# Batch 0's q in nine tokens per partition, as its k: two loads with longer rows, relu in halves, no separate tail

## Chip, cores and metric

The kernel runs on one core of one Trainium2 chip. The metric is the device time of one execution in microseconds (us), smaller is better. Each kernel was run several times; the text gives medians. A ratio is the mean time of one kernel's fast runs over that of the kernel before in the same rounds on the same chip, so not quite the ratio of the medians quoted.

## The reference

```python
def phi(x, c, s):                       # q and k: relu, then times cos and times sin
    r = np.maximum(x, 0.0)
    return np.concatenate([r * c, r * s], axis=-1)
kv  = einsum('bhsf,bhsd->bhfd', phi(k), v);  z = sum(phi(k), over tokens)
num = einsum('bhsf,bhfd->bhsd', phi(q), kv)
den = einsum('bhsf,bhf->bhs',   phi(q), z)[..., None] + 1e-6
x   = (num / den) as (4608 tokens, 512)         # 8 batches x 576 tokens, 8 heads x 64
xn  = x / sqrt(mean(x*x) + 1e-6) * rms_g
out = (silu(xn @ w_gate) * (xn @ w_val)) @ w_out        # 512 -> 1536 -> 512
```

q, k, v are float32 of shape (8, 8, 576, 64). The three matrix products of the last line are nearly all of TensorE's work. The scale c or s depends on the token alone.

## The kernel before

q is loaded with four tokens of one head per partition (512 of the 576 tokens), and the last 64 tokens, the tail, apart. k and v of batch 0 come with nine tokens per partition instead, as one contiguous run per partition. These loads all go through one queue (SyncE's) in the order of issue:

```python
def load_q_tokens(b, j0, j1):                   # before: 128 partitions x 8 heads
    view = q[b, :, 0:512, :].rearrange("h (p j) d -> p h j d", j=4)
    nc.sync.dma_start(out=raw[key][:, :, j0*D : j1*D],
                      in_=view[:, :, j0:j1, :].rearrange("p h j d -> p h (j d)"))
...
load_kv("k", 0, *LOW);  load_kv("k", 0, *HIGH)  # two halves of k
load_q_tokens(0, 0, 2)                          # q, tokens 0 and 1 of each four: 512 KB
first_v = load_kv("v", 0, *LOW)                 # ... then the rest of v in three loads
load_q_tokens(0, 2, 4)
```

Then, for a chunk c of 128 tokens of all heads: the relu with the scale (`q_phi`, once for cos on one engine and once for sin on the other), eight transposes on TensorE, an evacuation of the bank to SBUF, the product with kv and z (`nd_pe`), the division, the square and the norm (`x_sq`, `x_norm`), and the first products of the FFN:

```python
def q_phi(eng, b, c, part):
    src = view4(raw[("q", b)], c) if c < 4 else raw[("qt", b)][:, :, :]
    phi(eng, qp_tiles[(b, c)][:, :, o], src, f(c))          # one instruction of 512 elements
...                                                         # the opening, as issued:
    q_phi(A, 0, 2, 0); x_sq(0, 1)                           # chunk 2's relu ahead of a square
    ...
    q_phi(A, 0, 3, 1); q_tr_evac(A, 0, 2, psO[0][:, :])
    x_norm(0, 1)
    q_phi(V, 0, 3, 0)                                       # chunk 3's relu on DVE
    open_ffn(0, (0, 1), 0, 128)                             # the first FFN matmuls
    x_tr_pe(0, 1, psV[1][:, :]); x_tr_evac(V, 0, 1, psV[1][:, :])
    q_tr_pe(0, 3, psO[1][:, :])                             # chunk 3's transposes
```

In the profile's lines `phi` is L247 (ACT) and L249 (DVE), the copies and casts L316 and L318, the transposes of q L307, the first FFN matmuls L663. In the changed kernel the same lines are L252, L254, L337, L339, L321 and L692.

## Time and profile before

| | before |
|---|---|
| device time, first three runs | 327.01 us (326.49 to 327.02) |
| device time, six runs beside the changed kernel | 326.6 us (326.18 to 327.02) |
| profiled span | 325.4 us |
| PE busy / in the chain that ended last | 97% / 90% |
| first half of k, second half, q, first half of v land | 4.49, 6.03, 9.34, 10.86 us |
| first FFN matmul | 18.07 us |
| last weight load on PE, to the end of the span | 320.83 us, 4.62 us |

How to read it: PE works almost without a break from 18.07 us on, so a change in the opening can only move that start.

### The profile page before, as it was taken

To read this page: it belongs to the slowest core of one execution; us is meant where nothing else is said; L and a number is where in the kernel's file an instruction comes from. 1 tells how busy PE (TensorE), PEld (TensorE's weight loads), DVE (VectorE), ACT (ScalarE), POOL (GpSimd) and SP (SyncE) were. 2 spreads that over 40 slices of the span, in tenths; PEclk is the share of its full clock that TensorE was granted. 3 is DMA by queue.
4 is the path that set the end of the run, shared out by engine and by line. 5 is a ranking of instruction groups with operands and counts; after the bars stand their busy time and mean duration, and the time that the engine had idled before them with its cause. 6 is when DMAs were issued, how large, how long until landed. Compare 5 with 4: busy or idle time off the path is not lost.

```text
span 325.4 us, 6119 instructions
## 1 busy us (share of the span) xinstructions
PE 316.4 (97%) x2249; PEld 162.6 (50%) x2284; DVE 183.9 (57%) x394; ACT 173.4 (53%) x347; POOL 38.9 (12%) x85
## 2 busy tenths in 40 slices
PE   8999999999999999999999999999999999999994
PEld 3588465554445444554454445444544444444443
DVE  5875768787656765578267745772577143203310
ACT  6874775965665556645564466455654333233321
POOL 3570112001110110012001120120011000000000
PEclk9999999999999999999999999999999999999999
DMA  7999999887799665967597679766611400020014
GB/s 256 265 180 252 325 189 327 296 165 189 178 248 262 186 202 147 257 147 192 168 214 204 154 218 211 193 162 213 129 34 33 129 34 0 32 99 0 0 34 99
DMA packets 90881, 53.90 MB, mean 166 GB/s; under 512 B 56801, under 2 KB 83425, under 8 KB 90850
## 3 DMA queue, kind: packets, MB, share of 16 engines
q1 hardware_dynamic: 83808, 48.64, 57.3%
q0 software_dynamic: 6880, 4.72, 10.1%
q8 instruction: 18, 0.29, 0.4%
q10 hardware_dynamic: 162, 0.13, 0.2%
q14 instruction: 13, 0.11, 0.1%
HBM read 37.75 MB, written 9.44 MB: 145 GB/s over the span
## 4 chain that ended last, share of the span: by engine, by line
PE 90%; DMA 3%; ACT 2%; DVE 2%; issue 1%; SPq 0%; DVEq 0%
PE psC L544 26%; PE psV L524 26%; PE psG L524 26%; DMA rv<-in_v_dram 3%; PE psA L393 2%; PE psA L349 2%; PE psG L544 2%; PE psG L663 1%; PE psV L663 1%; PE psO L663 1%; PE psA L365 1%; ACT kpm L247 1%; PE psV L307 1%; ACT sg L533 0%; PE psA L400 0%
## 5 line engine op out<-in xcount | busy, mean ns | idle before, releaser
L539 DVE TENSOR_TENSOR hT<-psV,sg 128x512 bf16<-128x512 f32 x102 | 70.3, 689 | 95.9 <-PE psV L524 70.5
L533 ACT ACTIVATE sg<-psG 128x512 f32<-128x512 f32 x102 | 60.6, 594 | 64.9 <-PE psG L524 63.6
L524 PE MATMUL psV<-xnT,wv 128*128 128x512 bf16 (+1 forms) x365 | 92.1, 374 | 0.4
L524 PE MATMUL psG<-xnT,wg 128*128 128x512 bf16 (+1 forms) x352 | 90.8, 374 | 0.7
L544 PE MATMUL psC<-wo,hT 128*128 128x512 bf16 x382 | 88.2, 379 | 0.7
L524 PEld LDWEIGHTS <-wv 128*128 128x128 bf16 x416 | 40.6, 98 | 47.4
L544 PEld LDWEIGHTS <-hT 128*128 128x128 bf16 x420 | 40.3, 98 | 46.7
L524 PEld LDWEIGHTS <-wg 128*128 128x128 bf16 x416 | 38.6, 98 | 40.8 <-DVE xnT L318 0.4
L463 POOL TENSOR_TENSOR rs<-ms,mhalf 128x1 f32<-128x1 f32 x36 | 19.8, 549 | 187.9 <-ACT scr L458 187.9
L316 ACT COPY osb<-psC 128x512 f32<-128x512 f32 (+1 forms) x33 | 19.1, 578 | 43.4 <-PE psC L544 42.6
L485 DVE SCALAR_TENSOR_TENSOR xn<-xt,rs,gb 128x512 bf16<-128x512 f32 x35 | 26.5, 757 | 16.3 <-POOL rs L463 16.3
L458 ACT ACTIVATE scr<-xt 128x513 bf16<-128x513 f32 x36 | 22.8, 635 | 22.8 <-DVE xt L447 22.5
L247 ACT ACTIVATE kpm<-rk,tab 128x256 bf16<-128x256 f32 (+2 forms) x58 | 28.2, 545 | 1.7 <-DMA rk<-in_k_dram 1.7
L447 DVE TENSOR_TENSOR xt<-psA,rec 128x512 f32<-128x512 f32 x35 | 24.2, 691 | 1.2
L247 ACT ACTIVATE qp<-rq,tab 128x512 bf16<-128x512 f32 x32 | 22.4, 713 | 0.3 <-DMA rq<-in_q_dram 0.3
L249 DVE TENSOR_SCALAR kpm<-rk,tab 128x128 bf16<-128x128 f32 (+2 forms) x64 | 20.2, 374 | 2.3 <-DMA rk<-in_k_dram 2.3
L249 DVE TENSOR_SCALAR qp<-rq,tab 128x512 bf16<-128x512 f32 x32 | 15.3, 491 | 0.6 <-DMA rq<-in_q_dram 0.6
L393 PEld LDWEIGHTS <-qpT 128*128 128x128 bf16 x248 | 11.7, 98 | 6.7 <-issue 0.3
L393 PE MATMUL psA<-kvzs,qpT 128*128 128x65 bf16 x248 | 12.8, 193 | 0.3
L524 PE MATMUL psG<-xnt_tail,wg 128*128 128x512 bf16 x48 | 12.3, 379 | 0.1
L524 PE MATMUL psV<-xnt_tail,wv 128*128 128x512 bf16 x47 | 12.1, 379 | 0.0
L318 DVE CAST vvm<-rv 128x1024 bf16<-128x1024 f32 (+4 forms) x16 | 10.3, 670 | 0.2 <-DMA rv<-in_v_dram 0.2
(99 smaller groups left out, 184.3 us busy)
## 6 DMA issues: line engine op xcount, KB each, us to landing
out_dram<-osb SPq DMA_DIRECT2D x32, 256.0 KB, 2.6
rk<-in_k_dram SPq DMA_DIRECT2D x20, 256.0 KB, 3.4
rq<-in_q_dram SPq DMA_DIRECT2D x20, 256.0 KB, 3.0
rv<-in_v_dram SPq DMA_DIRECT2D x16, 256.0 KB, 3.1
rq<-in_q_dram SPq DMA_DIRECT2D x2, 1024.0 KB, 8.7
rv<-in_v_dram SPq DMA_DIRECT2D x3, 576.0 KB, 8.6
wo<-in_moe_w_out_dram POOLq DMA_DIRECT2D x4, 384.0 KB, 7.0
rk<-in_k_dram SPq DMA_DIRECT2D x2, 576.0 KB, 4.3
```

Of the source, the lines that this page charges most:

```text
L247: nc.scalar.activation(out=out_ap, in_=in_ap, func=AF.Relu, scale=scale)
L249: eng.tensor_scalar(out=out_ap, in0=in_ap, scalar1=scale, scalar2=0.0, op0=ALU.mult, op1=ALU.max)
L316: nc.scalar.copy(out=o, in_=i)
L393: nc.tensor.matmul(o[:, g, i, :], lhsT=qpT[(b, 0)][:, h, j * P : (j + 1) * P], rhs=kvz_of(b, h), start=True, stop=True,)
L447: nc.vector.tensor_tensor(out=xt[:, 0:DM].rearrange("p (b h d) -> p b h d", b=2, d=D), in0=o[:, :, :, 0:D], in1=rec[:, :, :].unsqueeze(3). ...
L458: nc.scalar.activation(out=scr[:, :], in_=xt[:, 0 : DM + 1], func=AF.Square, scale=1.0 / math.sqrt(DM), accum_out=ms[:, :],)
L463: nc.gpsimd.tensor_tensor(out=rs[:, :], in0=ms[:, :], in1=mhalf[:, :], op=ALU.pow)
L485: nc.vector.scalar_tensor_tensor(out=xn[:, :], in0=x_of[(b, j)][:, 0:DM], scalar=rs_of[(b, j)][:, :], in1=gb[:, :], op0=ALU.mult, op1=ALU. ...
L524: nc.tensor.matmul(pst[bank][:, cols[0] : cols[1]], lhsT=w[:, t, n * P : (n + 1) * P], rhs=x[:, t, cols[0] : cols[1]], start=(t == 0), sto ...
L533: nc.scalar.activation(out=sg[:, :], in_=psG[bank][:, :], func=AF.Silu)
L539: nc.vector.tensor_tensor(out=hTs[blk][:, n, :], in0=psV[bank][:, :], in1=sg[:, :], op=ALU.mult)
L544: nc.tensor.matmul(bank, lhsT=hTs[blk][:, n, j * P : (j + 1) * P], rhs=wo[:, n, :], start=(n == 0), stop=(n == NNT - 1),)
```

## The change

The intent: q of batch 0 in the layout of its k, so that its rows in DRAM are 1024 bytes (tokens 0 to 3 of nine) and 1280 bytes (tokens 4 to 8) instead of 512, and its tail needs no loads of its own. The price: a 64-row half of a chunk now holds another token, with another scale, so each relu becomes two instructions; the evacuation is strided; and block 0's rows are stored in eight pieces instead of four.

```diff
-    def load_q_tokens(b, j0, j1):
-        view = q[b, :, 0:512, :].rearrange("h (p j) d -> p h j d", j=4)
+    def load_q_tokens(j0, j1):
             out=raw[key][:, :, j0 * D : j1 * D],
-            in_=view[:, :, j0:j1, :].rearrange("p h j d -> p h (j d)"),
+            in_=q[0, :, :, :].rearrange("h s d -> (h s d)").rearrange(
+                "(r p n) -> p r n", p=P, n=NJ * D
+            )[:, :, j0 * D : j1 * D],
...
-    load_q_tokens(0, 0, 2)
+    load_q_tokens(0, 4)
     first_v = load_kv("v", 0, *LOW)
...
-    load_q_tokens(0, 2, 4)
+    load_q_tokens(4, NJ)
...  (q_phi)
+        if b == 0:
+            for i in range(2 if c < 4 else 1):
+                j = 2 * c + i
+                phi(eng, qp_tiles[(b, c)][:, 4 * i : 4 * i + 4, o],
+                    raw[("q", 0)][:, :, j * D : (j + 1) * D], f(5 + j))
+            return
...  (q_tr_evac, for b == 0)
+            src = bank.bitcast(BF16).rearrange("p (i h s) -> p h i s", i=2, h=H)
...  (out_store)
+        if blk == 0:
+            for i in range(2):
+                nc.sync.dma_start(out=rows0[2 * j + i, :, :], in_=osb[64*i : 64*i+64, :])
...  (after the first FFN steps; the loads of batch 0's tail at step 3 are gone)
+    q_phi(V, 0, 4, 0)
+    q_phi(A, 0, 4, 1)
```

More of the change, by code (lines that the diff above doesn't have):

```diff
@@ L90, in load_q @@
         if key not in raw:
-            raw[key] = one.tile([P, H, 4 * D], FP32, name="rq", tag="rq")
+            t = one.tile([P, 4, NJ * D], FP32, name="rq", tag="rq")
+            raw[key] = t[:, :, :].rearrange("p r n -> p (r n)")[:, 0 : H * 4 * D].rearrange(
+                "p (h n) -> p h n", h=H
+            )
         return nc.sync.dma_start(
@@ L143, in load_piece @@
             load_q_tail(b)
-    def load_q_tokens(b, j0, j1):
-        key = ("q", b)
+    def load_q_tokens(j0, j1):
+        key = ("q", 0)
         if key not in raw:
-            raw[key] = one.tile([P, H, 4 * D], FP32, name="rq", tag="rq")
-        view = q[b, :, 0:512, :].rearrange("h (p j) d -> p h j d", j=4)
+            raw[key] = one.tile([P, 4, NJ * D], FP32, name="rq", tag="rq")
         return nc.sync.dma_start(
             out=raw[key][:, :, j0 * D : j1 * D],
-            in_=view[:, :, j0:j1, :].rearrange("p h j d -> p h (j d)"),
+            in_=q[0, :, :, :].rearrange("h s d -> (h s d)").rearrange(
+                "(r p n) -> p r n", p=P, n=NJ * D
+            )[:, :, j0 * D : j1 * D],
         )
@@ L285, in q_phi @@
             )
+        if b == 0:
+            for i in range(2 if c < 4 else 1):
+                j = 2 * c + i
+                f = cos_of if part == 0 else sin_of
+                phi(
+                    eng, qp_tiles[(b, c)][:, 4 * i : 4 * i + 4, o],
+                    raw[("q", 0)][:, :, j * D : (j + 1) * D], f(5 + j),
+                )
+            return
         src = view4(raw[("q", b)], c) if c < 4 else raw[("qt", b)][:, :, :]
@@ L310, in q_tr_evac @@
         h0, h1 = heads if c < 4 else (0, 4)
+        if b == 0:
+            src = bank.bitcast(BF16).rearrange("p (i h s) -> p h i s", i=2, h=H)
+            copy(
+                eng, q_dst(b, c)[:, h0:h1, :].rearrange("p h (i s) -> p h i s", i=2),
+                src[:, h0:h1, :, :],
+            )
+            return
         dst = bank.bitcast(BF16).rearrange("p (h s) -> p h s", s=P)
@@ L399, in nd_pe @@
                     lo = 64 * (bb % 2)
+                    r, c = (h // 2, h % 2) if bb == 0 else (i, g)
                     nc.tensor.matmul(
                         o[lo : lo + 64, g, i, :],
-                        lhsT=qpT[(bb, 1)][:, i, 64 * g : 64 * g + 64],
+                        lhsT=qpT[(bb, 1)][:, r, 64 * c : 64 * c + 64],
                         rhs=kvz_of(bb, h), start=True, stop=True,
@@ L551, in out_store @@
         copy(eng, osb[:, :], bank)
-        if blk < 8:
+        rows0 = out[0:S, :].rearrange("(p j) m -> j p m", j=NJ)
+        if blk == 0:
+            for i in range(2):
+                nc.sync.dma_start(
+                    out=rows0[2 * j + i, :, :], in_=osb[64 * i : 64 * i + 64, :]
+                )
+        elif blk < 8:
             rows = out[blk * S : blk * S + 512, :].rearrange("(p j) m -> p j m", j=4)
@@ L558, in out_store @@
                 nc.sync.dma_start(
-                    out=out[r0 : r0 + 64, :], in_=osb[64 * i : 64 * i + 64, :]
+                    out=rows0[8, :, :] if i + j == 0 else out[r0 : r0 + 64, :],
+                    in_=osb[64 * i : 64 * i + 64, :],
                 )
@@ L874 @@
         if n == 3:
-            d = load_q_tail(0)
+            d = load_q_tail(1)
             tc.add_manual_dep(d.ins, wo_dmas[1].ins.name, SYNC_DEP, reason="after wo")
-            load_q_tail(1)
             load_kv("k", 2)
@@ L923 @@
     for bb in (0, 1):
-        at(1, 7 + bb, "post", q_phi, V, bb, 4, 0)
-        at(1, 7 + bb, "post", q_phi, A, bb, 4, 1)
+        if bb:
+            at(1, 7 + bb, "post", q_phi, V, bb, 4, 0)
+            at(1, 7 + bb, "post", q_phi, A, bb, 4, 1)
         at(1, 7 + bb, "post", q_tr_dma, bb, 4)
```

## The prediction

> **What bounds the kernel now.** I read the page first, then the chain of waits in order of time over the first 80 us, then the timeline, the landing times of the loads and the sizes of the DMA packets in the first 14 us.
>
> ```profile
> PE 316.4 (97%) x2249; PEld 162.6 (50%) x2284; DVE 183.9 (57%) x394; ACT 173.4 (53%) x347; POOL 38.9 (12%) x85
> ...
> PE 90%; DMA 3%; ACT 2%; DVE 2%; issue 1%; SPq 0%; DVEq 0%
> ```
>
> TensorE is busy for 97% of the span and carries 90% of the chain that ended last. The next view, busy time in windows (columns: stretch, its length, PE busy, granted clock, DMA share, GB/s), shows that there is almost nothing to win after the first 18 us:
>
> ```profile
> 18.10:30.80 12.70, 12.70 (x181) 1.00 1.31 230
> 30.80:321.00 290.20, 288.12 (x1921) 1.00 0.64 159
> ```
>
> From 18.1 to 30.8 us PE has no idle time at all, and in the 290.2 us after that only 290.2 - 288.1 = 2.1 us, nearly all of it in steps of about 53 ns that do not depend on this change. So the change can act only through the moment at which the unbroken PE work starts, 18.07 us. The chain of waits (start, length, what) tells what sets that moment:
>
> ```profile
> 1.75 0.47 SPq L151
> 2.23 0.04 issue
> 2.27 8.59 DMA rv<-in_v_dram
> 10.86 0.02 issue
> 10.88 0.68 ACT vvm L316
> ...
> 18.07 0.38 PE psG L663 x4
> ```
>
> The first half of v lands at 10.86 us because it queues behind k and behind the first half of q (L151). After it comes a fixed chain of 18.07 - 10.86 = 7.2 us (casts, kvz, normalisation, transposes). PE's matmuls before 10 us are fillers, not work. What ACT and DVE do beside it:
>
> ```profile
> 9.36 0.72 ACT L247 ACTIVATE qp<-rq,tab 128x512 bf16<-128x512 f32 x1 [0.30 <-DMA rq<-in_q_dram]
> 9.36 1.28 DVE L249 TENSOR_SCALAR qp<-rq,tab 128x512 bf16<-128x512 f32 x3 [0.57 <-DMA rq<-in_q_dram]
> ...
> 10.88 1.43 ACT L316 CAST vvm<-rv 128x576 bf16<-128x576 f32 x2 [0.33 <-DMA rv<-in_v_dram]
> 10.88 0.76 DVE L318 CAST vvm<-rv 128x576 bf16<-128x576 f32 x1 [0.24 <-DMA rv<-in_v_dram]
> ...
> 13.18 0.16 DVE L428 TENSOR_SCALAR rec<-psV 128x4 f32<-128x4 f32 x1 [0.21 <-PE psV L409]
> ```
>
> The idle times before q and v are small: 0.30 and 0.33 us on ACT, 0.57 and 0.24 us on DVE. The two engines are nearly a second bound here. However early q and v come, the opening cannot shrink by much more than these.
>
> **What the Trainium skill says.** (1) "DMA: Bandwidth & Descriptors", sections Specifications and "Why small descriptors are slow": line rate needs rows of 512 B or more, and each packet pays a fixed overhead. The packet records of this trace agree on the overhead but put the knee higher: in the undisturbed stretch a 512 B packet takes 28 ns (18 B/ns), 1024 B 46 ns, 1280 B 55 ns, 2304 B 94 ns (24.5 B/ns). (2) "Perfetto Trace Analysis", section "DMA Instruction — HWDGE": the issuing instruction's window is the generation of descriptors, not the movement. The trace agrees: the q load's instruction takes 0.47 us and its data lands 7.6 us after its start. (3) "ScalarE: Activation LUTs", section "What ACT_TABLE_LOAD costs": an ACTIVATE with one pointer operand takes about 280 ns + 0.833 ns per element, and neighbours overlap by 93 ns. That gives 706 and 493 ns for 512 and 256 elements; the rows below have 713 and 501. (4) "VectorE: DVE Perf Modes", section "Mode 2×_1P": two results per cycle for 16-bit data with step 1. The bf16 evacuations from PSUM agree: 679 ns for 1024 elements and 424 for 512, so 0.50 ns per element; the changed evacuation keeps step 1 in runs of 64.
>
> **The change part by part.**
>
> (a) First q load: 128 x 8 rows of 512 B become 128 x 4 rows of 1024 B, the same 512 KB. Packet time over 16 engines: 1024 x 28 / 16 = 1.79 us before, 512 x 46 / 16 = 1.47 us after. On the path: -0.32 us for q, and v behind it moves as much. There may be more. The second half of k lands at 1.25 + 4.8 = 6.05 us and q at 9.34, 3.3 us later, though its packets need 1.79; the three v loads behind then land after exactly their own packet times (1.52, 0.76, 0.45 us). The packet records show one or two of the 16 engines still on 512 B packets from 7.5 to 8.9 us when the others are through. If that straggling comes from the number of descriptors (1024 here, 256 in each k load, which do not straggle), half of them lets q land up to 1.8 us earlier, at about 7.5 us.
>
> (b) Relu of q, one instruction of 512 elements becomes two of 256. The rows by shape (last two numbers: busy us, mean ns):
>
> ```profile
> L247 ACT ACTIVATE qp<-rq,tab 128x512 bf16<-128x512 f32 x32 | 22.4, 713 | 0.3 <-DMA rq<-in_q_dram 0.3
> ...
> L247 ACT ACTIVATE kpm<-rk,tab 128x256 bf16<-128x256 f32 x23 | 10.4, 501 | 0.0
> ```
>
> ```profile
> L249 DVE TENSOR_SCALAR qp<-rq,tab 128x512 bf16<-128x512 f32 x32 | 15.3, 491 | 0.6 <-DMA rq<-in_q_dram 0.6
> ...
> L249 DVE TENSOR_SCALAR kpm<-rk,tab 128x256 bf16<-128x256 f32 x23 | 7.3, 358 | 0.0
> ```
>
> In a row, a 256 follows a 256 after 0.40 us on ACT and 0.26 us on DVE (runs of three: 1.29 and 0.87 us). Two of them take 0.50 + 0.40 = 0.90 us on ACT against 0.71, so +0.18 each, four times; on DVE 0.36 + 0.26 = 0.62 against 0.48, +0.13 each, four times. On the path before v: ACT +0.18, DVE 6 x 0.26 + 0.09 = 1.65 us against 1.28, +0.37. The ACT pair for chunk 2 (from 14.37) falls into ACT's later wait of 0.26 us; the one at 16.00 delays the next square by about 0.2 us, which PE, then busy with the first tokens' FFN, mostly hides.
>
> Sum up to kvz. If q lands only 0.32 us earlier, at 9.02: DVE is through with q at 9.04 + 1.65 = 10.69 and casts v then instead of at 10.88 (-0.19); ACT is through with q and the gain row at about 10.5 and casts from 10.56 (-0.32). The gain is 0.2 us. If q lands at 7.5: DVE starts at 8.79 when k is done, ends at 10.43 (-0.45); ACT starts at 9.07, ends at about 10.45 (-0.43). The gain is 0.45 us and then the engines set it. The rest of the 7.2 us chain moves along, minus up to 0.1 us for the later halves of the split.
>
> (c) Second q load: 512 rows of 1280 B, 512 x 55 / 16 = 1.76 us against 1024 x 30 / 16 = 1.9. It has 128 KB more, lands no later, and is first needed at 14.37. 0.
>
> (d) Tail of batch 0: two loads of 64 KB go at 33 to 45 us, its relu moves from about 71 us to about 26 us, where ACT stands idle for 1.98 us and DVE for 1.45. Both lie beside a full PE. 0.
>
> (e) Stores of block 0: eight of 64 rows for four of 128, at 56 to 59 us; four more issues of some 0.35 us on SyncE. What queues behind is not needed for tens of us. 0.
>
> Total -0.2 to -0.45, less 0.1: about -0.3 us. 327.0 - 0.3 = 326.7; as the three runs before lie between 326.5 and 327.0, I put 326.6.
>
> **Rivals.** *The wait moves from DMA to ACT and DVE, and nothing is left* (the splits cost DVE 0.37 us before v, and the wait removed is 0.24 + 0.57): for it speak the small idle times; against it, that k's relu ends at 8.79, so q can be taken up earlier. It would give 326.9 to 327.1. *The strided evacuation or the narrower relu loses its doubled rate*: a cast of 128x576 on DVE took 758 ns, 128x1152 only 751, so the rate does hang on shape. At half the rate the evacuation at 11.55 would take 0.5 us more on DVE's path: 327.2 to 327.5. Against it: the new relu has the shape of k's, which has the good rate. *A large gain*, if everything follows v by 1.8 us: 325.2. Against it: k's relu ends at 8.79 and 9.07 and then 1.4 to 1.6 us of work stand before the casts.
>
> **Range and chances.** The bounds of my sum are -0.45 and 0; the spread of equal runs is 0.5 us. So 325.9 to 327.2. A change of 2% is 6.5 us, while all PE idle time that the change could reach is some 1.5 us between 11.3 and 18.1 plus the shift of v: faster 0.005, slower 0.01, within 2% 0.985.
>
> **What the profile will show.** Right: q lands well before 9.34 and the v casts start at 10.4 to 10.7; the first FFN matmul at 17.6 to 17.9; DVE without idle time between k's relu and the v cast; the evacuation still about 0.68 us; PE busy time after 18 us unchanged. If q lands near 7.5 us, the straggling hung on the number of descriptors; if near 9.0, only the packet time counted. The prediction is wrong if the first FFN matmul does not come earlier, if the evacuation takes over 1 us, or if new PE gaps open after 40 us, where transfers come in another order.

## More of the kernel before

One more stretch is needed later, the timeline round chunk 3 (start, duration in us, engine, line, operation, tiles, shapes, count, and in brackets idle time and what ended it):

```profile
17.40 0.55 POOL L463 TENSOR_TENSOR rs<-ms,mhalf 128x1 f32<-128x1 f32 x1 [0.65 <-ACT scr L458]
...
17.98 0.75 DVE L485 SCALAR_TENSOR_TENSOR xn<-xt,rs,gb 128x512 bf16<-128x512 f32 x1
...
18.65 0.48 DVE L249 TENSOR_SCALAR qp<-rq,tab 128x512 bf16<-128x512 f32 x1
...
18.68 0.76 POOL L231 DMA_DIRECT2D wv<-in_moe_w_val_dram  x1
...
18.96 0.39 PE L510 MATMUL psV<-ident,xn 128*128 128x128 bf16 x4
19.28 0.61 PE L307 MATMUL psO<-ident,qp 128*128 128x128 bf16 x8
```

DVE's norm starts at once, chunk 3's relu follows and ends at 19.13, and PE goes through all eight transposes of chunk 3 without a wait.

## The result, and the profile after

The changed kernel took 326.34 us (326.17 to 326.95, six runs), the kernel before 326.6 us in the same rounds (326.18 to 327.02, six runs). The ratio is 0.9994 with a 95% interval of 0.9981 to 1.0007: the same, by the clock. The point predicted was 326.6 us, the range 325.9 to 327.2, and 0.985 on "within 2%". The number held. The point is also what the kernel before took beside it, so by itself it does not tell the predicted gain of 0.3 us from none. The steps behind it did not all hold, and the rest of this document is about them.

The page of the changed kernel (busy time of the engines; share of the chain that ended last):

```profile
PE 316.2 (97%) x2249; PEld 162.4 (50%) x2284; DVE 184.3 (57%) x398; ACT 173.8 (54%) x351; POOL 39.3 (12%) x85
...
PE 93%; DVE 2%; ACT 2%; issue 1%; POOL 0%; DVEq 0%
...
rq<-in_q_dram SPq DMA_DIRECT2D x1, 512.0 KB, 6.5
```

The load of v, 3% of the chain before, is gone from it; the share of PE went from 90% to 93%. The third line is the first q load: 6.5 us from issue to landing, against 7.6 before. Busy time in windows, with the columns of the prediction's:

```profile
18.10:30.80 12.70, 12.48 (x171) 1.00 1.30 232
30.80:321.00 290.20, 287.97 (x1920) 1.00 0.64 158
```

Between 18.1 and 30.8 us PE now misses 0.22 us, where it missed nothing before. After that there is next to no change (2.23 us missed against 2.08). The timeline where q and v arrive:

```profile
8.47 1.66 DVE L254 TENSOR_SCALAR qp<-rq,tab 128x256 bf16<-128x256 f32 x6
8.73 0.89 ACT L252 ACTIVATE qp<-rq,tab 128x256 bf16<-128x256 f32 x2
...
10.05 0.75 DVE L339 CAST vvm<-rv 128x576 bf16<-128x576 f32 x1
10.07 1.25 ACT L337 CAST vvm<-rv 128x576 bf16<-128x576 f32 x2
10.71 0.68 DVE L339 COPY qpT<-psV 128x1024 bf16<-128x1024 bf16 x1
```

No line has a wait in brackets any more: q landed at 8.26 and v at 9.77, and DVE and ACT came to them later than that. They are the bound of this stretch. The last line is the strided evacuation, 0.68 us as before. And round chunk 3:

```profile
16.77 0.55 POOL L485 TENSOR_TENSOR rs<-ms,mhalf 128x1 f32<-128x1 f32 x1 [0.84 <-ACT scr L480]
...
17.26 0.38 PE L692 MATMUL psG<-xnT,wg 128*128 128x128 bf16 x4 [0.35 <-ACT xnT L337]
17.36 0.75 DVE L507 SCALAR_TENSOR_TENSOR xn<-xt,rs,gb 128x512 bf16<-128x512 f32 x1
...
18.03 0.89 DVE L254 TENSOR_SCALAR qp<-rq,tab 128x256 bf16<-128x256 f32 x2
18.05 0.75 POOL L236 DMA_DIRECT2D wv<-in_moe_w_val_dram  x1
...
18.17 0.40 PE L532 MATMUL psV<-ident,xn 128*128 128x128 bf16 x4
18.52 0.38 PE L321 MATMUL psO<-ident,qp 128*128 128x128 bf16 x4
...
19.07 0.38 PE L321 MATMUL psO<-ident,qp 128*128 128x128 bf16 x4 [0.16 <-DVE qp L254]
```

The first FFN matmul came 0.81 us earlier than in the profile before (17.26 against 18.07). But the eight transposes of chunk 3 fell into two groups: the second waited for DVE. From there on PE was ahead by only 0.43 us, and that stayed so to its last weight load (320.40 against 320.83). So half of the gain was given back within 2 us.

The profiled span shrank by 0.97 us, of which PE accounts for 0.43. The other 0.53 us came after the last weight load, where this change does nothing on purpose: from there to the end of the program it is 4.62 us before and 4.09 after. And the timed runs show less than either. Three questions therefore: does q really land earlier, what did the split cost, and what happened at the end?

### The profile page after: what moved, and what is told of

It reads as the page before. It is cut to its first block, busy times and chain, and to the rows that moved or that the text cites. A ratio compares the mean times of both kernels' runs of the same rounds, so it can differ in the third digit from the quotient of the medians.

```text
span 324.5 us, 6131 instructions
## 1 busy us (share of the span) xinstructions
PE 316.2 (97%) x2249; PEld 162.4 (50%) x2284; DVE 184.3 (57%) x398; ACT 173.8 (54%) x351; POOL 39.3 (12%) x85
## 4 chain that ended last, share of the span: by engine, by line
PE 93%; DVE 2%; ACT 2%; issue 1%; POOL 0%; DVEq 0%
PE psC L566 26%; PE psV L546 26%; PE psG L546 26%; PE psA L414 2%; PE psO L593 2%; PE psA L370 2%; PE psG L566 2%; PE psO L692 1%; PE psG L692 1%; PE psV L692 1%; PE psV L321 1%; ACT kpm L252 1%; PE psA L386 1%; ACT sg L555 0%; PE psA L422 0%
## 5 line engine op out<-in xcount | busy, mean ns | idle before, releaser
L252 ACT ACTIVATE qp<-rq,tab 128x512 bf16<-128x512 f32 (+1 forms) x37 | 23.7, 661 | 0.0
L254 DVE TENSOR_SCALAR qp<-rq,tab 128x512 bf16<-128x512 f32 (+1 forms) x37 | 16.0, 452 | 0.0
L339 DVE CAST vvm<-rv 128x1024 bf16<-128x1024 f32 (+4 forms) x16 | 10.4, 674 | 0.0
```

The costliest lines, as they stand in the source:

```text
L252: nc.scalar.activation(out=out_ap, in_=in_ap, func=AF.Relu, scale=scale)
L254: eng.tensor_scalar(out=out_ap, in0=in_ap, scalar1=scale, scalar2=0.0, op0=ALU.mult, op1=ALU.max)
```

## The experiments

Twelve runs were made, of eight kernels. Theory A is that the lateness of q comes from the number of rows in its load, theory C that the split of the relu costs PE time at chunk 3, theory E that the number of transfers sets the length of the end. Milestones of all traces are collected in one table, after the runs. "q lag" is the landing of q less that of the second half of k, just ahead in the queue. "Opening" is from the landing of the first half of k to the first FFN matmul. "Chunk 3" is from that matmul to the weight load of the second half of chunk 3's transposes. "End" is from the last weight load to the end of the span.

**before_again, after_again, before_third, after_third.** Both kernels as they are, for the spread.

> A second profile of the kernel before, unchanged, to tell luck from effect. In the first pair of profiles the first half of k landed at 4.49 us before and 4.25 us after, although nothing ahead of it differs. Theory A (the straggling of one DMA engine in the q load comes from its 1024 rows): q lands again about 3.3 us (3.0 to 3.6) after the second half of k, v 1.52 us after q, first FFN matmul near 18.1 us. Rival B (the straggling is an accident of one run): q lands 1.8 to 2.5 us after k this time. The landing of the first half of k is expected to vary by 0.2 to 0.3 us either way.

> A second profile and five more timed rounds of the changed kernel, unchanged. Time against the kernel before: -0.1 to -0.5 us (ratio 0.9985 to 0.9997). Trace: q lands 2.3 to 2.7 us after the second half of k (theory A), v cast on DVE begins without a wait within 0.05 us of the end of q's relu; first FFN matmul at 17.2 to 17.6 us, and by 30 us PE is only 0.3 to 0.5 us ahead of the kernel before, because the transposes of chunk 3 wait for DVE at about 19 us.

> The kernel before once more, for q's landing after the second half of k on the same chip as the next two. So far 3.31 and 2.82 us. Theory F (1024 rows in one load cost the packet time and an accident of 0.8 to 1.5 us that any large load meets here): 2.6 to 3.4 us.

> The changed kernel once more, on the same chip. With these loads q's lag so far was 2.50, 2.28, 2.93 and 2.87 us. Theory F: 2.2 to 3.0 us, on average 0.15 to 0.4 us under the kernel before; the accident stays.

Measured: before_again 326.81 us and before_third 326.37 (one run each), after_third 326.19 (one run); after_again 326.6 (326.25 to 327.43, five runs), ratio 1.0004 (0.9990 to 1.0017). So the second timing of the change has it as slow as before. The expectation for after_again, a gain of 0.1 to 0.5 us, was missed. The traces tell why the first profile looked so good: q landed at 9.34, 8.91 and 8.43 us in the three profiles of the kernel before, at 8.26, 8.13 and 8.48 in those of the change. The profile in the prediction was the unluckiest of its kind. In before_again the lag, 2.82 us, lies between what theory A and its rival B had put down; on the one chip of before_third and after_third the change's lag was the longer one (2.71 against 2.40), against the expectation.

**rows_512, rows_256, rows_512_again.** The changed kernel, its first q load in two loads with rows of 512 bytes, or four with rows of 256.

```diff
-    load_q_tokens(0, 4)
+    load_q_tokens(0, 2)          # rows_512
+    load_q_tokens(2, 4)
-    load_q_tokens(0, 4)
+    for j in range(4):           # rows_256
+        load_q_tokens(j, j + 1)
```

> The changed kernel, but the first q load fetched as two loads of two tokens each: the same 512 KB to the same places, in 1024 rows of 512 B in place of 512 rows of 1024 B; a right result. Packet time alone: 1.79 us in place of 1.47, so the second of the q loads and v land 0.3 us later relative to the second half of k than in the changed kernel (2.8 us after it). Theory A (the number of rows makes one engine straggle): about 3.3 us after it, as in the kernel before. If the layout in memory was what counted (the addresses that neighbouring rows have), 2.5 us, as in the changed kernel.

> As before, but four loads of one token each: 2048 rows of 256 B. A packet of 256 B takes some 19 to 20 ns by the two sizes measured (28 ns for 512 B, 46 for 1024), so 2.5 us for the load: packet time alone puts q at 3.5 us after the second half of k. Theory A: the straggling grows with the number of rows, so 4.5 to 6 us. The opening gets longer than before the change: first FFN matmul at 19 to 21 us.

> The 1024 rows of 512 B in two loads once more, on the same chip as the two before it. Its lag was 2.19 us on another chip. If the chip made the difference, it is now 2.6 to 3.4 us as in the kernel before. If two smaller loads are what avoids the straggling, it is again near 2.2 us, less than the changed kernel's, although its packets take longer.

Measured: 326.37, 327.25 and 326.17 us, one run each; the kernel before took 327.91 in its one run beside the first two. The q lag was 2.19 and 2.62 us with 512-byte rows in two loads, 2.32 with 256-byte rows, against 2.28 to 2.97 in the six profiles with 1024-byte rows. Each lag is below every figure that was put down for it, but for the 2.62 of the repeat, which is at the edge of "the chip made the difference". Twice or four times the rows did not make q later. **Theory A falls.** The packet records show what rows do cost: the time of q's packets, summed and divided by 16 engines, is

```
rows of     packets   packet, median   sum / 16, us                    q lag, us, one load
 256 bytes    2048        18 ns         2.55                            (four loads: 2.32)
 512 bytes    1024        27 ns         1.77 to 1.84  (5 runs)          2.40 to 3.31, mean 2.78
1024 bytes     512        46 ns         1.58 to 1.79  (6 runs)          2.28 to 2.97, mean 2.71
```

With 1024 bytes the median packet is 46 ns, but the mean is 49 to 56, as some were slow at 5 to 6.5 us. On the mean of the runs (1.81 and 1.69) the packets save 0.12 us, and the lag falls by 0.07 us, within a spread of 0.7 to 0.9. In rows_256 q itself was not late, but SyncE issued v late. Its issues, from the timeline:

```profile
1.75 2.13 SPq L154 DMA_DIRECT2D rq<-in_q_dram  x4
3.92 3.31 SPq L82 DMA_DIRECT2D rv<-in_v_dram  x4
```

The first v load was issued at 3.92 instead of 2.27 us, stood 1.85 us in its issue, and landed 2.0 us after q. What makes a few of the 16 engines, in the end one or two, lag up to a microsecond behind, in some runs more than in others, stays open.

**split_only.** The kernel before with only the relu of batch 0's q split in two, same values.

```diff
+        if b == 0 and c < 4:
+            for i in range(2):
+                hs = slice(4 * i, 4 * i + 4)
+                phi(eng, qp_tiles[(b, c)][:, hs, o], src[:, hs, :], f(c))
+            return
         phi(eng, qp_tiles[(b, c)][:, :, o], src, f(c))
```

> The kernel before with one part of the change alone: each relu of a full q chunk of batch 0 as two instructions of 256 elements (over two halves of the heads); loads and layout as before, a right result. Theory C: from the first FFN matmul to the transposes of chunk 3 PE loses 0.3 to 0.45 us that the kernel before does not lose (1.75 us between the two in place of 1.38), and the casts of v start up to 0.15 us later after q's landing; time 0.3 to 0.6 us over the kernel before, ratio 1.001 to 1.002. Rival D (the cost came with the layout, not with the split): 1.38 us as before, ratio 1.000.

Measured: 326.91 us (326.8 to 327.19, six runs) against 326.57 of the kernel before; ratio 1.0009 (0.9996 to 1.0023), so +0.3 us, not clear of zero by the clock. The trace is clearer: chunk 3 takes 1.78 us, as in the changed kernel, and the same two lines stand there:

```profile
18.03 0.89 DVE L249 TENSOR_SCALAR qp<-rq,tab 128x256 bf16<-128x256 f32 x2
...
19.06 0.38 PE L312 MATMUL psO<-ident,qp 128*128 128x128 bf16 x4 [0.16 <-DVE qp L249]
```

**one_relu.** The reverse: the changed layout with one relu instruction per chunk, which gives the odd tokens the wrong scale.

```diff
-            for i in range(2 if c < 4 else 1):
-                j = 2 * c + i
-                phi(eng, qp_tiles[(b, c)][:, 4*i : 4*i+4, o], raw[("q", 0)][:, :, j*D : (j+1)*D], f(5 + j))
+            n = 2 if c < 4 else 1
+            phi(eng, qp_tiles[(b, c)][:, 0 : 4*n, o].rearrange("p (i r) d -> p i r d", i=n),
+                raw[("q", 0)][:, :, 2*c*D : (2*c+n)*D].rearrange("p r (i d) -> p i r d", i=n), f(5 + 2*c))
```

> The changed kernel with the two 256-element relu instructions of each q chunk of batch 0 put together into one of 512 (one scale for both tokens, so a wrong result on purpose). Everything else stays. Theory C (the split relu takes back about 0.37 us at chunk 3 and holds the v casts): the six DVE instructions before v become three, 1.28 us in place of 1.66, the casts of v then wait for the DMA again or start about 0.3 us earlier relative to k's landing, the 0.16 us PE gap at 19 us is gone, and at 30 us PE is 0.3 to 0.6 us further ahead than in the changed kernel; time 325.7 to 326.1. Rival D (something else in the new layout, such as the strided evacuation, takes it back): PE at 30 us is where it is in the changed kernel, within 0.1 us, and the time is 326.3.

Measured: 326.09 us (325.72 to 326.34, four runs), ratio 0.9981 (0.9966 to 0.9997). Chunk 3 takes 1.38 us, as before, and the casts of v wait for the load again (0.26 us on DVE). One thing that was put down for theory C did not come: PE was to be 0.3 to 0.6 us further ahead than in the changed kernel, but its last weight load came at 320.43 us against 320.31 to 320.40, which is what rival D had put down. In this execution v landed at 10.46 us, 0.5 to 0.8 us later than in the three profiles of the change. As the landings move that much between executions, the stretch of chunk 3, which begins after them, is the test, and by it rival D falls. Undoing the split takes the loss away, doing it alone brings it: **theory C holds**. The loss is 1.78 - 1.38 = 0.40 us in every one of the seven profiles with the split as the change has it, against all five without it.

How the 0.40 us comes about can be added up from the timelines of before and after, relative to the first FFN matmul. ACT's split of chunk 2's relu (0.89 us at 15.19) delays the square behind it, so POOL's `rs` and DVE's norm: the norm starts 0.10 us after that matmul, where in the kernel before it started 0.09 us ahead of it. Chunk 3's relu on DVE starts 0.19 us later with it, and its pair takes 0.89 us instead of 0.48; its end moves by 0.19 + 0.41 = 0.60 us. In the kernel before PE came 0.32 us after the end of that relu, in the changed one 0.12 us after it. So there were 0.20 us of slack, and 0.60 - 0.20 = 0.40 is what PE loses.

Of the 0.41 us by which the pair is longer, 0.28 are its second half alone, which takes 0.63 us instead of 0.35. The POOL lines of the two stretches round chunk 3 show what stands beside it: POOL issues the loads of the FFN weights, some 0.75 us each. In the changed kernel the second half starts 0.24 us into such an issue and ends 0.12 us after it; the single relu of the kernel before started 0.02 us ahead of one and kept its 0.48 us. Over all 14 traces, 40 of the 506 relus of 256 elements on DVE take over 0.37 us. Each of the 40 began inside an instruction of POOL's: 28 inside a cast, 12 inside the issue of a load, and these 12 ended 0.09 to 0.12 us after the issue did. So the second half was most likely held up by POOL; no run tests that alone. Without the hold the loss would be 0.19 + 0.13 - 0.20 = 0.12 us, an estimate from these numbers.

**early_chunk3, early_again.** The changed kernel with DVE's relu of chunk 3 issued before the evacuation of the first tokens' transposes, in a place where DVE is idle for about 0.5 us.

```diff
     x_scale(0, 0)
+    q_phi(V, 0, 3, 0)
...
     x_norm(0, 1)
-    q_phi(V, 0, 3, 0)
```

> The changed kernel with DVE's two relu instructions of q chunk 3 moved ahead, to the 0.49 us in which DVE waits for the transposes of the first x tile; all else the same, a right result. Theory C: PE no longer waits at chunk 3's transposes, the first FFN matmul is at most 0.1 us later, and at 30 us PE is 0.25 to 0.4 us ahead of the changed kernel; time 325.8 to 326.1, ratio to the kernel before 0.998. Rival D: the wait at 19 us only moves to the next matmul and PE at 30 us is where it was; time 326.3.

> The repeat of the changed kernel with DVE's relu of chunk 3 ahead of the evacuation of the first tokens' transposes, on another occasion and beside other runs of the kernel before. If the 0.6 us of early_chunk3 was more than the luck of one job: ratio 0.998 to 0.999, 325.9 to 326.3 us, first FFN matmul to the second half of chunk 3's transposes 1.38 to 1.55 us against the 1.78 of the change (1.38 if the first slice of the value weights lands before it is asked for, more by what it comes late), the end 4.07 to 4.10. If it was luck: ratio 1.000, as after_again had.

Measured: 326.0 us (325.94 to 326.44, five runs), ratio 0.9986 (0.9973 to 0.9999); the second time, on another chip, 326.13 us (325.98 to 326.61, six runs), ratio 0.9977 (0.9964 to 0.9991). Chunk 3 takes 1.55 and 1.59 us instead of 1.78, just over the bracket that I gave for the second. The wait for DVE is gone, and PE has found another one. From the timeline of early_again:

```profile
16.77 0.61 DVE L254 TENSOR_SCALAR qp<-rq,tab 128x256 bf16<-128x256 f32 x2
...
18.17 0.23 PEld L693 LDWEIGHTS <-wv 128*128 128x128 bf16 x4 [0.30 <-DMA wv<-in_moe_w_val_dram]
...
19.08 0.61 PE L321 MATMUL psO<-ident,qp 128*128 128x128 bf16 x8
```

The relu pair, at the free place, takes the 0.61 us that the prediction had worked out, where the old place took 0.89 (POOL issues no load beside it here). The eight transposes are one group again. ACT's evacuation, which in the changed kernel ended at 18.91 like DVE's relu, is not what they wait for: here they run from 19.08 on while it lasts to 19.31. But the first slice of the value weights is late by 0.30 us. In the three profiles of the change that slice had landed 0.3 to 1.2 us before it was asked for, so whether this wait belongs to the new order or to these two executions is not shown.

Two expectations for early_chunk3 failed. The first FFN matmul was to be at most 0.1 us later than in the change; it came at 17.64 and 17.66 us against 17.18 to 17.26. And PE was to be 0.25 to 0.4 us ahead; its last weight load came at 320.58 and 320.72 us, 0.2 to 0.4 us behind the change's 320.31 to 320.40. In these two executions v landed at 10.43 and 10.45 us, and both were the slowest timed ones of their run (326.44 and 326.61 us). The gain of the new order rests on chunk 3 and on the clock, not on these milestones.

**tail_two_more.** The kernel before with two of block 0's stores split into halves, so two more transfers on SyncE, as the change has two more; the layout of q untouched.

```diff
-            nc.sync.dma_start(out=rows[:, j, :], in_=osb[:, :])
+            for r0 in (0, 64) if blk == 0 and j < 2 else (0,):
+                r1 = r0 + 64 if blk == 0 and j < 2 else P
+                nc.sync.dma_start(out=rows[r0:r1, j, :], in_=osb[r0:r1, :])
```

> The kernel before with two stores of block 0 (two of its four j) split into two stores of 64 rows each, so two more transfers on SyncE, as the change has two more; result right, nothing else altered. The end of the program, from the last LDWEIGHTS to the end of the span, was 4.61 to 4.62 us in all four profiles with the layout of before (split_only among them) and 4.07 to 4.10 in all profiles of the change. Theory E (the number of transfers sets where the last landing falls in the row of semaphore waits at the end): the end becomes other than 4.61, most likely about 4.1, with PE unchanged (first FFN matmul to the second half of chunk 3's transposes 1.38 us, the last LDWEIGHTS at 320.0 to 320.8), and the time goes to about 326.1, ratio about 0.9985. Rival (the end is set by the changed layout itself, for instance by its last stores or its loads, not by the number of transfers): the end stays 4.61 and the ratio is 1.000.

Measured: 326.16 us (326.02 to 326.52, six runs) against 326.77 (326.36 to 328.04, eleven runs), ratio 0.998 (0.9965 to 0.9995), right result. The end takes 4.09 us, as with the change, and chunk 3 takes 1.38. **Theory E holds**: 0.53 us of the span came from two more transfers some 260 us earlier; with three and five more, loads of q in rows_512 and rows_256, the end was another again (4.01 and 4.75).

The records of SyncE's semaphore instructions show the place. At the end SyncE takes nine waits, one after another. "Perfetto Trace Analysis", section "Sequencer-only Instruction (DRAIN, etc)", of the Trainium skill says that such an instruction's reported start is the moment at which its semaphores are satisfied; the trace agrees, as in every kernel one of the nine starts at 3.03 to 3.05 us, when the last store is through. Starts in us after the last weight load:

```
                 SyncE transfers   nine waits of the end (the last landing in brackets)              end
before                210          1.33 1.39 1.71 1.90 [3.05] 3.12 3.19 3.26 3.65                    4.62
after                 212          1.33 1.39 1.45 1.52 1.70 1.87 [3.03] 3.11 3.17                    4.09
tail_two_more         212          1.33 1.39 1.45 1.52 1.72 1.90 [3.03] 3.11 3.17                    4.09
rows_512              213          1.34 1.41 1.48 1.55 1.62 2.01 2.10 [3.04] 3.10                    4.01
rows_256              215          1.33 [3.04] 3.11 3.50 3.58 3.65 3.71 3.77 3.84                    4.75
```

Two more transfers move the last landing from the fifth wait to the seventh, three to the eighth, five to the second, which fits a rotation by eight. What stands behind it in the row is paid after it, about 0.07 us each and one step of 0.39 us where that falls behind it too. What that step is stays open.

All milestones (us; the runs of the kernel before first, then those with the split, then the rest):

| profile | first half of k | q lag | first FFN matmul | opening | chunk 3 | end |
|---|---|---|---|---|---|---|
| before | 4.49 | 3.31 | 18.07 | 13.58 | 1.38 | 4.62 |
| before_again | 4.47 | 2.82 | 17.64 | 13.17 | 1.37 | 4.61 |
| before_third | 4.45 | 2.40 | 17.19 | 12.74 | 1.38 | 4.61 |
| tail_two_more | 4.46 | 2.61 | 17.38 | 12.92 | 1.38 | 4.09 |
| split_only | 4.27 | 2.77 | 17.25 | 12.98 | 1.78 | 4.62 |
| after | 4.25 | 2.50 | 17.26 | 13.01 | 1.78 | 4.09 |
| after_again | 4.33 | 2.28 | 17.26 | 12.93 | 1.78 | 4.08 |
| after_third | 4.23 | 2.71 | 17.18 | 12.95 | 1.78 | 4.10 |
| rows_512 | 4.38 | 2.19 | 17.31 | 12.93 | 1.78 | 4.01 |
| rows_512_again | 4.31 | 2.62 | 17.24 | 12.93 | 1.77 | 4.01 |
| rows_256 | 4.34 | 2.32 | 17.52 | 13.18 | 1.78 | 4.75 |
| one_relu | 4.34 | 2.93 | 17.67 | 13.33 | 1.38 | 4.09 |
| early_chunk3 | 4.47 | 2.87 | 17.64 | 13.17 | 1.55 | 4.07 |
| early_again | 4.45 | 2.97 | 17.66 | 13.21 | 1.59 | 4.07 |

The table leaves one thing out. The first half of k, which no edit touches and which was issued at 0.73 to 0.74 us everywhere, landed at 4.45 to 4.49 us in the profiles of the kernel before, tail_two_more and the reordered change, and at 4.23 to 4.38 in the eight others. That goes with the program more than with chance, it is worth 0.2 us, and no run explains it. Counted as a gain of the change it would bring the change's sum below to -0.4, outside the interval of after_again. In the same way the three profiles of the change have q lags of 2.28 to 2.71 us and the three with the same loads but another relu, or another place of it, 2.87 to 2.97.

The opening of the four profiles with the old layout and no split is 13.10 us on the mean; that of the five profiles of the change and of its reordered form is 13.05. So the layout, with its price of splits included, bought 0.05 us there, under a spread of 0.8 and 0.3, so not clear of zero (0.14 with the change's own three profiles alone). With that the terms agree with what the clock says (each measured as its ratio less 1, times 326.6 us, with the interval in brackets):

| kernel | opening | chunk 3 | end | sum | measured |
|---|---|---|---|---|---|
| the change, first timing | -0.05 | +0.40 | -0.53 | -0.2 | -0.2 (-0.6 to +0.2) |
| the change, after_again | -0.05 | +0.40 | -0.53 | -0.2 | +0.1 (-0.3 to +0.6) |
| split_only | not separable | +0.40 | 0 | +0.4 | +0.3 (-0.1 to +0.8) |
| one_relu | not separable | 0 | -0.53 | -0.5 | -0.6 (-1.1 to -0.1) |
| early_chunk3 | -0.05 | +0.17 | -0.53 | -0.4 | -0.5 (-0.9 to 0.0) |
| early_again | -0.05 | +0.21 | -0.53 | -0.4 | -0.8 (-1.2 to -0.3) |
| tail_two_more | 0 | 0 | -0.53 | -0.5 | -0.7 (-1.1 to -0.2) |

Every sum lies within its interval. tail_two_more and the reordered change are both faster than the kernel before, by 0.1 to 0.2%: within the 2% that counts as the same here, but with intervals clear of 1. Against the change itself they stand at 326.16, 326.0 and 326.13 us to 326.34 and 326.6, though only early_chunk3 and after_again (and one_relu, 326.09) were taken in the same rounds. The two gains were not put together in one kernel.

## Why the prediction was right, and where its steps were not

The time fell into the range because the bounds were right: PE's idle time after 18 us leaves nothing to win, and the engines beside PE close the opening. Step by step:

- **The bound (right).** After 30.8 us PE is as busy as before (287.97 against 288.12 us), and its lead of 0.43 us stays constant to the end.
- **(a) The first load: the size failed.** The packets save 0.12 us, not 0.32, since packets of 1024 bytes held their 46 ns only in the median. "If that straggling comes from the number of descriptors" was put as a condition; it does not. The lag changes from run to run by 0.7 to 0.9 us in either layout. The prediction took one profile's 9.34 us for the kernel's, and it was the latest of five.
- **(b) The relu before v: right.** Six on DVE took 1.66 us (predicted 1.65), the pair on ACT 0.89 (0.90). And the engines set the time: in all three profiles of the change DVE and ACT reach q and v with no wait, and the casts start at 10.00 to 10.13, where the kernel before had 10.00 to 10.88. That holds only where q comes early: in one_relu, early_chunk3 and early_again q landed at 8.9 us, v at 10.43 to 10.46, and the casts started at 10.45 to 10.53, as in before_again (q 8.91, casts 10.44).
- **(b) The later splits: the step that failed.** "Minus up to 0.1 us for the later halves" was 0.40, four times as much. The prediction named the delayed square and then let PE's FFN work hide it. It overlooked that chunk 3's transposes stand on PE in front of the rest of that FFN work (18.52 and 19.07 us in the profile after), and that the relu they need is on DVE behind the delayed norm. It also took the pair at 0.62 us, which it takes at the free place of early_again (0.61), while beside POOL's issue of a load it took 0.89. Without that it would have been about right (0.12 us, estimated above).
- **(c), (d), (e): right.** The second load is needed late; the tail's relu (0.52 us on ACT, 0.34 on DVE, at 25 to 27 us) and the eight stores of block 0 left PE's lead where it was. But with two loads fewer and four stores more, (d) and (e) raised the number of transfers from 210 to 212, and their "0" does not hold for the end of the program.
- **Evacuation: right.** 0.68 us on DVE, 1.00 on ACT, so the second rival falls. The third, a gain of 1.8 us, falls with theory A. The first rival, that the wait moves to ACT and DVE and nothing is left, describes the opening best: 0.05 us was left.
- **What was missing.** The end of the program, -0.53 us, was in no step. Without it the sum is -0.05 + 0.40, a loss of some 0.3 us. The prediction came to about the right number because two errors, some 0.3 us too hopeful on the load and 0.3 on the split, were made up by an omission of 0.5. That is luck.
- **What the profile was to show.** The casts came earlier than the 10.4 to 10.7 that I gave, and the first FFN matmul at 17.26 instead of 17.6 to 17.9, as k landed 0.24 us earlier in that run besides. A new PE gap did open, at 18.9 us and not after 40.

## What to carry to other kernels

Take the landing times of several profiles before crediting a change with an earlier landing: here one load moved by 0.9 us between equal runs, more than the change could win. When an instruction on a side engine is split or delayed, follow it to the first instruction on the bounding engine that needs it, in that engine's own order, rather than calling it hidden because the engine is busy. And look at the end of the span apart from the work: an edit that only alters the number of transfers can move the time by 0.5 us, which is easily taken for the worth of the edit.

## What the Trainium skill lacked or had wrong

- "DMA: Bandwidth & Descriptors", Specifications, has 512 bytes as the smallest transfer for line rate. Here 512 bytes in 27 ns are 19 bytes/ns per engine, 1024 in 46 ns are 22, and 2304 in 93 ns are 24.8 (medians), so 512 is not yet the full rate, and the packets cost 1.81 against 1.69 us for the same 512 KB on the mean.
- No page looked up has the spread of a single load's landing: 2.40 to 3.31 us after the load ahead of it in five profiles of one and the same pattern.
- No page looked up has that a program's end depends on the number of its transfers: nine semaphore waits of SyncE one after another, 4.01 to 4.75 us from the last weight load to the end with 210 to 215 transfers, in a way that fits a rotation of eight.
